# Building rows of `yv` for two more chunks by batch: four column groups in single rounds, and most gather copies on ScalarE

## The chip, the cores and the metric

The kernel runs on one core of a Trainium2 chip. The metric is the device time of one execution in microseconds (us). Two kernels are compared by executions of the same rounds on the same chip. "Span" is the length of one profiled execution, some 2 us shorter than its time.

## The reference, cut to what matters

Causal attention with a decaying bias feeds a spectral mix: 64 Fourier modes of the sequence are multiplied by complex weights of 512 x 512 each, transformed back and added to the input; then comes a product with `w_ch` and a ReLU.

```python
def _moe_ref(x, w_r, w_i, w_ch):               # x is the attention's output, (8, 576, 512)
    X = np.fft.rfft(x, axis=1)
    Xr, Xi = np.real(X[:, :64]), np.imag(X[:, :64])
    Yr = einsum('bmd,mde->bme', Xr, w_r) - einsum('bmd,mde->bme', Xi, w_i)
    Yi = einsum('bmd,mde->bme', Xr, w_i) + einsum('bmd,mde->bme', Xi, w_r)
    y = np.fft.irfft(Y, n=S, axis=1)           # Y holds Yr + 1j*Yi for 64 modes, else 0
    u = x + y
    return u + np.maximum(u @ w_ch, 0.0)
```

(The arrays `w_r` and `w_i`, 64 x 512 x 512 in float32, are most of what is read from memory.)

## The kernel before

The 64 modes go in eight chunks of eight, `c` = 0 to 7. All chunk numbers in this text and in the prediction are these, counted from zero. For the last quarter of the model dimension (`g = NG - 1`) each chunk's modes product gives `y_sb`, 128 rows = 16 real and imaginary modes x 8 batches. The inverse transform needs these rows, and their product with `w_ch`, ordered by mode within a batch: the tile `yv` (128 modes; batch; 0 for y and 1 for y@w_ch; 512). There are two ways to get them there.

By chunk, `y_times_wch`: one product of 128 rows, a copy to `v_sb`, and a transfer of 128 KB that spreads the rows over the batches.

```python
def spread(c, which, rows):
    nc.sync.dma_start(out=yv[16 * c : 16 * c + 16, :, which, :], in_=rows)

def y_times_wch(c, yt):
    vp = auxpool.tile([P, DM], FP32, name="v_ps", tag="aux")     # auxpool: PSUM, 2 buffers
    # ... 4 matmuls of yt (128 x 128) with wch_sb
    vb = spool.tile([P, DM], FP16, name="v_sb", tag="v")
    nc.vector.tensor_copy(out=vb, in_=vp)
    spread(c, 1, vb)
    return vb
```

By batch, `gather`: the transposed rows of several chunks lie in `yt_first`; a matmul takes one batch's columns of them as weights, so its result has the right order already. Several batches stand side by side in column groups of one PSUM tile, and each group is copied into `yv` by itself.

```python
def gather(c0, c1, turns, kinds):
    n = 2 * MC * (c1 - c0)            # 64 rows for chunks 0 to 3, 32 for 4 and 5
    ng = P // n                       # groups side by side: 2 or 4
    for b0 in range(0, B, ng):
        for which in kinds:           # 0: identity, gives y; 1: wch_sb, gives y@w_ch
            ps = auxpool.tile([P, DM], FP32, name="g_ps", tag="aux")
            # ... 4 x ng matmuls with tile_position=(0, n * g)
            for g in range(ng):
                dst, src = yv[rows, b0 + g, which, :], ps[n * g : n * g + n, :]
                if g % 2:
                    nc.vector.tensor_copy(out=dst, in_=src)
                else:
                    nc.scalar.copy(out=dst, in_=src)
        # ... if b0 // ng in turns: work()
```

Before, chunks 0 to 3 go by batch altogether; chunks 4 and 5 go by batch for y alone (identity) and by chunk for y@w_ch; chunks 6 and 7 go by chunk. The order of it (`work()` is an independent product of x with `w_ch`, to fill TensorE):

```python
for c in range(NCK - 2):
    yb = modes(NG - 1, c)
    # ... work(); x_transposed(0) in chunk 5
    yt = y_transposed(yb, c)
    # ... work()
    if c >= NY:                                  # chunks 4 and 5
        y_times_wch(c, yt)
        if c == NCK - 3:
            gather(NY, NCK - 2, (), (0,))
    elif c == NY - 1:
        gather(0, NY, (1, 3), (1, 0))
c = NCK - 2                                      # chunk 6
x_times_wch(0, False)
yb6 = modes(NG - 1, c)
x_transposed(1)
yt = y_transposed(yb6)
x_times_wch(1, False)
vb6 = y_times_wch(c, yt)
# ... chunk 7: modes in four quarters, with first_u and first_z between them
```

The modes product, the transposes, `v_ps` and `g_ps` all use the two buffers of `auxpool`, a pool in PSUM, the memory that the products of TensorE are written to here. Weights stream in all the time through transfers that GpSimd issues; SyncE issues those into `yv` and the results.

The softmax here doesn't subtract the row's maximum and nothing guards it: scores larger than these inputs give would overflow.

## Time and profile before

| what | before |
|---|---|
| time, median of 3 | 456.47 us (455.56 to 456.91) |
| profiled span | 453.8 us (time 455.52) |
| chunk four's modes product starts | 390.79 |
| last quarter of chunk seven's starts | 415.30 |
| from there to the end | 38.50 |

Lines of a time line read: start (us), duration, engine, source line, operation, out<-in, shape in partitions x elements, type, count of instructions in a row; in brackets the idle time ahead of it and who ended it. The prediction below shows TensorE and VectorE of the stretch that is edited. ScalarE's side of the same gather of chunks four and five, which the prediction uses for its spacing:

```profile
402.29 0.57 ACT L664 CAST yv<-g_ps 32x512 f16<-32x512 f32 x1 [0.27 <-PE g_ps L652]
403.61 1.17 ACT L664 CAST yv<-g_ps 32x512 f16<-32x512 f32 x2 [0.75 <-DVE yv L662]
405.66 0.58 ACT L664 CAST yv<-g_ps 32x512 f16<-32x512 f32 x1 [0.88 <-DVE yv L662]
```

Four copies of 32 rows each (one batch's), about 0.58 us apiece; the two in a row took 1.17 together, and between them ScalarE waits for VectorE's copies of the same tile.

### The profile page before, as it was taken

To read this page: it belongs to the slowest core of one execution; us is meant where nothing else is said; L and a number is where in the kernel's file an instruction comes from. 1 tells how busy PE (TensorE), PEld (TensorE's weight loads), DVE (VectorE), ACT (ScalarE), POOL (GpSimd) and SP (SyncE) were. 2 spreads that over 40 slices of the span, in tenths; PEclk is the share of its full clock that TensorE was granted. 3 is DMA by queue.
4 is the path that set the end of the run, shared out by engine and by line. 5 is a ranking of instruction groups with operands and counts; after the bars stand their busy time and mean duration, and the time that the engine had idled before them with its cause. 6 is when DMAs were issued, how large, how long until landed. Compare 5 with 4: busy or idle time off the path is not lost.

```text
span 453.8 us, 10370 instructions
## 1 busy us (share of the span) xinstructions
PE 340.4 (75%) x4233; PEld 218.6 (48%) x4265; DVE 241.0 (53%) x535; ACT 221.9 (49%) x390; POOL 183.0 (40%) x269
## 2 busy tenths in 40 slices
PE   1779887976563979836677857688889678879995
PEld 1456665654342656624445535456554335534332
DVE  7775665753242656723436434446655443562796
ACT  1585877464242656724435444455551323431774
POOL 6655554554344565434364444444433231200000
PEclk9996999998576889968878899889996986999999
DMA  9999999999999999999999999999999999995688
GB/s 176 200 203 203 202 201 204 202 204 204 205 204 202 201 203 202 205 205 204 202 196 203 204 204 203 204 203 202 206 207 208 207 206 206 207 214 109 232 298 317
DMA packets 108511, 93.75 MB, mean 207 GB/s; under 512 B 28384, under 2 KB 103648, under 8 KB 108464
## 3 DMA queue, kind: packets, MB, share of 16 engines
q0 software_dynamic: 98960, 81.81, 113.8%
q1 hardware_dynamic: 9504, 11.29, 7.8%
q8 instruction: 33, 0.54, 0.4%
q14 instruction: 14, 0.11, 0.1%
HBM read 164.56 MB, written 9.44 MB: 383 GB/s over the span
## 4 chain that ended last, share of the span: by engine, by line
DMA 51%; PE 31%; DVE 8%; issue 4%; POOL 2%; ACT 2%; SPq 0%; DVEq 0%; POOLq 0%; ACTq 0%
DMA w_sb<-in_moe_w_i_dram 21%; DMA q<-in_q_dram 15%; DMA w_sb<-in_moe_w_r_dram 11%; PE sc_ps L365 4%; PE av_ps L394 4%; PE z_ps L602 3%; PE yp L441 3%; PE sc_ps L359 3%; PE tr_ps L324 3%; DMA k<-in_k_dram 2%; PE z_ps L693 2%; PE g_ps L652 2%; PE ft_ps L418 2%; PE u_ps L712 2%; PE u_ps L693 1%
## 5 line engine op out<-in xcount | busy, mean ns | idle before, releaser
L373 ACT ACTIVATE p_sb<-sc_ps,cumt_sb 128x576 f16<-128x576 f32 (+1 forms) x256 | 141.7, 635 | 45.6 <-PE sc_ps L365 45.0
L217 POOL DMA_DIRECT2D w_sb<-in_moe_w_i_dram x60 | 45.1, 751 | 85.0 <-PE yp L441 37.6
L217 POOL DMA_DIRECT2D w_sb<-in_moe_w_r_dram x60 | 45.3, 757 | 63.5 <-DMA w_sb<-in_moe_w_r_dram 28.2
L217 POOL DMA_DIRECT2D v<-in_v_dram x72 | 50.8, 708 | 32.0 <-DMA w_sb<-in_moe_w_r_dram 7.4
L324 PE MATMUL tr_ps<-ident,q 64*64 64x64 bf16 x576 | 17.5, 210 | 54.3 <-DMA q<-in_q_dram 54.3
L359 PE MATMUL sc_ps<-negm,ident 128*128 128x256 bf16 x256 | 55.5, 303 | 0.2
L327 DVE COPY qtA<-tr_ps 64x576 bf16<-64x576 bf16 x32 | 23.8, 743 | 49.6 <-PE tr_ps L324 49.5
L441 PE MATMUL yp<-w_sb,xs 128*32 128x512 bf16 x480 | 36.5, 406 | 14.1 <-DMA w_sb<-in_moe_w_i_dram 11.1
L344 ACT ACTIVATE p<-sc_ps,cumt 128x64 f16<-128x64 f32 x32 | 10.0, 313 | 74.3 <-PE sc_ps L340 74.3
L394 PE MATMUL av_ps<-v,p_sb 128*128 128x65 f16 x1024 | 44.5, 198 | 0.0
L394 PEld LDWEIGHTS <-p_sb 128*128 128x128 f16 x1024 | 39.5, 100 | 4.9 <-issue 0.8
L327 DVE COPY ktA<-tr_ps 64x576 bf16<-64x576 bf16 x32 | 24.0, 749 | 33.6 <-PE tr_ps L324 33.6
L324 PEld LDWEIGHTS <-q 64*64 64x64 bf16 x576 | 13.7, 123 | 57.0 <-DMA q<-in_q_dram 56.3
L365 PE MATMUL sc_ps<-qtB,ktB 128*128 128x64 bf16 (+2 forms) x160 | 34.9, 324 | 3.5 <-issue 2.4
L365 PE MATMUL sc_ps<-qtA,ktA 65*128 65x512 bf16 (+2 forms) x192 | 36.5, 299 | 0.7 <-DMA qtA<-ncum_sb 0.7
L399 DVE TENSOR_REDUCE den<-av_ps 128x5 f32<-128x10 f32 x64 | 10.8, 169 | 49.1 <-PE av_ps L394 48.9
L441 PEld LDWEIGHTS <-xs 128*32 128x32 bf16 x512 | 22.6, 170 | 23.8 <-issue 19.8
L404 DVE TENSOR_TENSOR x_all<-av_ps,rcp 128x320 f16<-128x320 f32 x64 | 31.5, 491 | 2.2
L327 ACT COPY ktB<-tr_ps 64x576 bf16<-64x576 bf16 x32 | 20.3, 634 | 20.3 <-DVE ktA L327 19.4
L365 PEld LDWEIGHTS <-ktB 128*128 128x128 bf16 x192 | 22.4, 117 | 14.8 <-issue 6.3
L324 PE MATMUL tr_ps<-ident,k 64*64 64x64 bf16 x576 | 17.3, 209 | 15.3 <-DVE qtB L327 10.7
L602 PE MATMUL z_ps<-wch_sb,xs 128*128 128x512 f16 x96 | 26.1, 421 | 0.2 <-DVE xs L596 0.2
(117 smaller groups left out, 534.8 us busy)
## 6 DMA issues: line engine op xcount, KB each, us to landing
w_sb<-in_moe_w_r_dram POOLq DMA_DIRECT2D x60, 512.0 KB, 11.9
w_sb<-in_moe_w_i_dram POOLq DMA_DIRECT2D x60, 512.0 KB, 11.9
q<-in_q_dram POOLq DMA_DIRECT2D x32, 144.0 KB, 9.9
k<-in_k_dram POOLq DMA_DIRECT2D x32, 144.0 KB, 10.0
v<-in_v_dram POOLq DMA_DIRECT2D x72, 64.0 KB, 9.7
out_dram<-r_sb SPq DMA_DIRECT2D x16, 256.0 KB, 2.2
out_dram<-r_w SPq DMA_DIRECT2D x16, 256.0 KB, 2.6
x_all<-in_moe_w_i_dram POOLq DMA_DIRECT2D x3, 512.0 KB, 9.9
```

The lines of the kernel that those rows point to most:

```text
L217: nc.gpsimd.dma_start(out=dst, in_=src)
L324: nc.tensor.transpose(ps[rows, r, :], src[rows, r, :], ident16[rows, rows])
L327: copy(out=dst[n % NQ][rows, :].rearrange("d (p r) -> d p r", r=R), in_=ps[rows].rearrange("d r p -> d p r"),)
L359: nc.tensor.matmul(ps[:, bass.ds(w * S, W)], ident16, negm[:, bass.ts(r, W)], start=True, stop=False, skip_group_check=True,)
L365: nc.tensor.matmul(ps[:, c0 : c0 + i1 - i0], keys[:, w, r, :], qt[:, i0:i1], start=False, stop=True, skip_group_check=True,)
L373: nc.scalar.activation(out=pt[:, poff[x] : poff[x] + S - w * W], in_=ps[:, w * S : (w + 1) * S - w * W], func=ACTF.Exp, bias=cumt_sb[:, x, ...
L394: nc.tensor.matmul(ps[:, I, r : r + NCH], lhsT, rhs, start=(i == 0), stop=(i == len(todo) - 1), skip_group_check=True,)
L399: nc.vector.tensor_reduce(out=den, in_=ps[:, :, 0 : VW : NCH], axis=mybir.AxisListType.X, op=ALU.add)
L404: nc.vector.tensor_tensor(out=x_all[:, g, b, :, D * h : D * h + D], in0=ps[:, :, 1 : NCH], in1=rcp.unsqueeze(2).to_broadcast([P, NT, D]), ...
L441: nc.tensor.matmul(ps[32 * cg : 32 * cg + 32, :], cols[:, c0 : c0 + 32, c * MC + 2 * cg + par], wt[(g, c, ri, par)][:, cg, :], start=(x == ...
L602: nc.tensor.matmul(z[:, x, :], xts[i][:, x, dt, :], wch_sb[:, dt, :], start=(dt == 0), stop=(last and dt == DT - 1), skip_group_check=True,)
L693: nc.tensor.matmul(dst[x][r, :], G_sb[rows, bass.ds(T * P, r.stop - r.start)], yv[rows, bb, which, :], start=start, stop=True, skip_group_ ...
```

## The change

The intent is to send y@w_ch of chunks four and five the way of the other chunks: by batch, in four column groups, so that two products, two VectorE copies and two transfers of 128 KB go away. The rounds are no longer made in one place but singly, between other products, where TensorE was waiting for `y_sb`. And in every gather only the last copy of a tile is VectorE's, so that VectorE is free for `y_sb`. Cut to its core:

```diff
-    def gather(c0, c1, turns, kinds):
+    def gather(c0, c1, r, which):          # one round r, one kind
...
-                    if g % 2:
+            if g == ng - 1:
                 nc.vector.tensor_copy(out=dst, in_=src)
             else:
                 nc.scalar.copy(out=dst, in_=src)
...
-        if c >= NY:
-            y_times_wch(c, yt)
-            if c == NCK - 3:
-                gather(NY, NCK - 2, (), (0,))
-        elif c == NY - 1:
-            gather(0, NY, (1, 3), (1, 0))
+        if c == NY - 1:
+            for r in range(4):
+                gather(0, NY, r, 1)
+                gather(0, NY, r, 0)
+                if r % 2:
+                    work()
+        elif c == NCK - 3:
+            gather(NY, NCK - 2, 0, 1)
+            gather(NY, NCK - 2, 0, 0)
     c = NCK - 2
     x_times_wch(0, False)
+    gather(NY, NCK - 2, 1, 1)
     yb6 = modes(NG - 1, c)
     x_transposed(1)
+    gather(NY, NCK - 2, 1, 0)
     yt = y_transposed(yb6)
```

More of the change, by code (lines that the diff above doesn't have):

```diff
@@ L645, in gather @@
         ng = P // n
-        for b0 in range(0, B, ng):
-            for which in kinds:
-                ps = auxpool.tile([P, DM], FP32, name="g_ps", tag="aux")
-                for dt in range(DT):
-                    for g in range(ng):
-                        op = yt_first[:, dt, : c1 - c0].rearrange("p c (x b) -> p (c x) b", b=B)
-                        nc.tensor.matmul(
-                            ps[n * g : n * g + n, :] if which else ps[n * g : n * g + n, bass.ts(dt, P)],
-                            op[:, :, b0 + g],
-                            wch_sb[:, dt, :] if which else ident16h,
-                            start=(dt == 0 or not which), stop=(dt == DT - 1 or not which),
-                            tile_position=(0, n * g), skip_group_check=True,
-                        )
-                for g in range(ng):
-                    dst, src = yv[rows, b0 + g, which, :], ps[n * g : n * g + n, :]
-                    if g % 2:
-                        nc.vector.tensor_copy(out=dst, in_=src)
-                    else:
-                        nc.scalar.copy(out=dst, in_=src)
-            if b0 // ng in turns:
-                work()
+        ps = auxpool.tile([P, DM], FP32, name="g_ps", tag="aux")
+        op = yt_first[:, :, : c1 - c0].rearrange("p d c (x b) -> p d (c x) b", b=B)
+        for dt in range(DT):
+            for g in range(ng):
+                nc.tensor.matmul(
+                    ps[n * g : n * g + n, :] if which else ps[n * g : n * g + n, bass.ts(dt, P)],
+                    op[:, dt, :, r * ng + g],
+                    wch_sb[:, dt, :] if which else ident16h,
+                    start=(dt == 0 or not which), stop=(dt == DT - 1 or not which),
+                    tile_position=(0, n * g), skip_group_check=True,
+                )
+        for g in range(ng):
+            dst, src = yv[rows, r * ng + g, which, :], ps[n * g : n * g + n, :]
+            if g == ng - 1:
+                nc.vector.tensor_copy(out=dst, in_=src)
+            else:
+                nc.scalar.copy(out=dst, in_=src)
     ahead = []
```

## The prediction

> **What bounds the kernel now.** I read the page's slices first, then the chain of waits, then the last 80 us engine by engine, then the landing times of the last weight loads.
>
> The page: the DMA engines stand at nine tenths or more from the first slice to slice 36 of 40, and the chain of waits gives 51% of the span to DMA, nearly all of it weight and query loads.
>
> ```profile
> DMA  9999999999999999999999999999999999995688
> DMA 51%; PE 31%; DVE 8%; issue 4%; POOL 2%; ACT 2%; SPq 0%; DVEq 0%; POOLq 0%; ACTq 0%
> ```
>
> So the kernel streams weights until about 415 us, and a tail of some 38 us after that needs no loads. The change touches neither: it sits between chunk four (its modes product starts at 390.79) and the last quarter of chunk seven (415.30). The windows of that stretch (us; PE, PEld, DVE, ACT, POOL busy; clock; DMA share, GB/s):
>
> ```profile
> 390.80:396.10 5.30, 4.49 (x45) 2.39 (x44) 2.62 (x5) 2.38 (x3) 2.97 (x4) 1.00 1.24 207
> 396.10:405.00 8.90, 7.39 (x85) 3.82 (x84) 5.74 (x9) 3.56 (x6) 0.74 (x1) 1.00 1.23 211
> 405.00:411.00 6.00, 4.70 (x40) 2.35 (x40) 3.21 (x5) 1.16 (x2) 0.00 (x0) 1.00 1.23 214
> 411.00:415.80 4.80, 4.78 (x31) 1.83 (x30) 0.69 (x1) 0.00 (x0) 0.00 (x0) 1.00 0.56 116
> ```
>
> TensorE is busy 78 to 85% up to 411 and all of the time from 411 to 415.8, at full clock; that is its in-order stream with a few gaps. TensorE in order of time, cut to what the change touches:
>
> ```profile
> 395.13 1.03 PE L633 MATMUL v_ps<-wch_sb,yt_first 128*128 128x512 f16 x4
> 396.08 1.12 PE L441 MATMUL yp<-w_sb,xs 128*32 128x512 bf16 x16
> ...
> 398.85 0.40 PE L625 MATMUL yt_ps<-ident16h,y_sb 128*128 128x128 f16 x4 [1.09 <-DVE y_sb L455]
> ...
> 402.61 0.47 PE L652 MATMUL g_ps<-ident16h,yt_first 128*32 128x128 f16 x16 [0.38 <-DVE v_sb L637]
> ...
> 407.75 0.40 PE L625 MATMUL yt_ps<-ident16h,y_sb 128*128 128x128 f16 x4 [1.10 <-DVE y_sb L455]
> 408.34 1.90 PE L602 MATMUL z_ps<-wch_sb,xs 128*128 128x512 f16 x8 [0.20 <-DVE xs L596]
> ...
> 415.30 0.47 PE L441 MATMUL yp<-w_sb,xs 128*32 128x512 bf16 x4
> ```
>
> The gaps of 1.1 us are waits for `y_sb`, the modes result copied out by VectorE. Why it is late for chunk six is in VectorE's stream: it is queued behind the gather's copies, which alternate with ScalarE's.
>
> ```profile
> 402.89 0.69 DVE L662 CAST yv<-g_ps 32x512 f16<-32x512 f32 x1 [0.33 <-ACT yv L664]
> 404.22 1.41 DVE L662 CAST yv<-g_ps 32x512 f16<-32x512 f32 x2 [0.64 <-ACT yv L664]
> 406.27 0.69 DVE L662 CAST yv<-g_ps 32x512 f16<-32x512 f32 x1 [0.64 <-ACT yv L664]
> 407.00 0.69 DVE L455 TENSOR_TENSOR y_sb<-yp,y_acc 128x512 f16<-128x512 f32 x1
> ```
>
> Last, the load that the 415.30 product needs. It is issued at 396.87 and lands 18.3 us later, at 415.17, so it is 0.13 us early; the product starts right behind its predecessor. TensorE's order and the DMA stream meet within 0.2 us there. This is the fact the prediction turns on.
>
> ```profile
> 396.87 0.74 POOL L217 DMA_DIRECT2D w_sb<-in_moe_w_i_dram  x1 [2.15 <-PE yp L441]
> w_sb<-in_moe_w_i_dram POOLq DMA_DIRECT2D x1, 512.0 KB, 18.3
> ```
>
> **What the skill says.** The Trainium skill, "TensorEngine Tiling (Array Packing)", Performance Considerations, says that tiling speeds TensorE but not the emptying of PSUM, which may become the bottleneck. The trace agrees: two rounds of 16 identity products took 0.41 us each, their eight copies 402.29 to 406.96. "PSUM — Partial Sum Buffer", PSUM bank collisions, says that two engines on one bank must be kept apart, reads against reads included, though quadrants differ freely. Here the schedule separates them by the whole tile: each VectorE copy above starts after the ScalarE copy of the same tile, although they read different quadrants. "DMA: Bandwidth & Descriptors", Issuing engines are not separate DMA queues, says that transfers from all queues share the same 16 engines; the landings of the weights below agree.
>
> **The change part by part.** Everything up to chunk four keeps its order: the first gather has two groups per round, so its copies are one on ScalarE and one on VectorE as before.
>
> Removed: for chunks four and five, two products of 4 matmuls (next start 0.95 us after the first's start, 0.80 to 0.95 of the path each, say 1.8 us of TensorE), two VectorE copies `v_sb` of 0.69 us, and two SyncE transfers of 128 KB into `yv`.
>
> Added: two rounds of 16 matmuls with 32 weight columns and 512 columns out. The modes product has the same form, x16 in 1.12 us, its successor 1.05 after its start; so 2 x 1.05 = 2.1 us. So TensorE gets 0.3 us more work, not less. Each new round is also emptied by four copies of 32x512: eight more copies. All 16 copies now stand as 12 on ScalarE and 4 on VectorE, that is +8 and 0; with the two `v_sb` gone VectorE saves 1.4 us, ScalarE gains 8 x 0.58 = 4.6 us. ScalarE has 1.16 to 3.56 us of work in windows of 6 to 9 us, so it has room; a tile of four takes 3 ScalarE copies and one VectorE copy behind them. Two ScalarE copies in a row took 1.06 (64x512) and 1.17 us (32x512) together, one alone 0.58, thus they start 0.48 (overlapping) to 0.59 apart; with 0.48 a tile is freed 2 x 0.48 + 0.58 + 0.69, about 2.3 us, after its product is readable.
>
> Moved: rounds one (product, identity) stand before the first late `z_ps` product, round two's product behind it, round two's identity behind chunk six's modes product. All use the same two auxiliary PSUM buffers as the modes product and the transposes, so each waits for the copies of the tile two back.
>
> I put this on one time line, keeping the distances that the trace shows (modes product start to `y_sb` 1.18, `y_sb` to transposes 0.74, `z_ps` product 1.73, its `ScalarE` copy 1.93 after its start):
> - Modes of five start at 395.13, not 396.08 (no `v_ps` before). But VectorE is in the 1.22 us subtraction begun at 396.37, so `y_sb` starts at 397.51, not 398.11, and the transposes at 398.25: 0.6 gained.
> - `z_ps` 398.48 to 400.21; round one's product to 401.26, its identity to 401.67, the next `z_ps` to 403.40. Copies of tile one: ScalarE 401.39 to 402.93, VectorE to 403.66; of tile two: to 405.1.
> - Round two's product waits 0.33 for tile one: 403.73 to 404.78. Chunk six's modes waits 0.39 for tile two: 405.17, against 404.97 before. The gain is used up.
> - Round two's VectorE copy (406.49 to 407.18) is ahead of `y_sb` of six, which starts at 407.09, against 407.00. The identity round hides in that gap (407.25 to 407.66). Transposes 407.83, `z_ps` 408.43, `v_ps` 410.17 (its buffer free 410.02), chunk seven's modes 411.13, against 411.04.
> - From there 4.26 us of solid TensorE work as before: 415.39 against 415.30.
>
> With ScalarE copies 0.59 apart, and thus later releases, the same line gives about 415.8. So TensorE's path: +0.1 to +0.5 us.
>
> The DMA side gains: landings of the last six weight loads are 400.8, 404.28, 406.2, 409.3, 412.0, 415.17, that is 14.37 us for five, where undisturbed ones come each 2.54 us (512 KB at 206 GB/s): 12.7. The 1.67 us extra fit the four 128 KB transfers in that time, about 0.63 us each, the last only partly. Two go away: the last weight lands near 413.9 (estimate), 1.3 us earlier, and nothing is there to use it. It only sets the floor: at best 415.30 - 413.9, thus 1.4 us gained.
>
> After 415.4 nothing differs. Sum: near 0, from -1.4 to +0.5.
>
> **Rivals.** (1) The rounds fill TensorE's waits fully, because copies go faster than I think or the stalls for the buffers vanish: then chunk seven waits for its weights and the gain is capped at 1.3 us: 455.1. For it: all three waits of 1.1 us are there to be filled, and the arrangement looks made for it. Against: two buffers for four more users. (2) ScalarE's serial copies hold the buffers and delay chunk six: +0.5 to +1 us, 457.2. For it: each tile now needs 3 copies of one engine, and they also queue ahead of the copy of chunk six's transposes. Against: ScalarE is only about 40% busy there. (3) Fewer transfers let all weights land earlier and the end moves with them. Against: the product at 415.30 does not wait in the trace.
>
> **Range and chances.** The before runs spread over 455.56 to 456.91, 1.35 us, as much as the whole effect. The middle of my line is +0.1 to +0.5; the first rival pulls the other way by up to 1.3. I take 0.2 us off for the chance of it and set 456.3. The range takes both rivals and half the spread of the runs: 454.8 to 457.4. A change of 2% is 9 us, seven times the cap; faster 0.01, same 0.98, slower 0.01.
>
> **What would show it.** In the changed profile: the start of the last quarter of chunk seven's modes at 415.3 +- 0.6; the last weight landing about 1.3 us before it instead of 0.1; waits of TensorE for `yv` copies in round two and chunk six's modes, 0.3 to 0.4 us each; `y_sb` of five about 0.6 earlier, `y_sb` of six about unchanged; the stretch from there to the end within 0.3 us of 38.5. Wrong would be: that last quarter waiting for its weights (rival 1), a start later than 416 (rival 2), or a difference that arises before 390 us or after 415 us.

## More of the kernel before

Behind the last weight load, the first product that reads all 128 rows of `yv` (`128*128`; earlier ones read 96 rows) follows TensorE's previous work with no wait:

```profile
421.12 1.03 PE L827 MATMUL z_ps<-r_sb,ident16h 128*128 128x512 f16 x4
421.99 0.59 PE L693 MATMUL z_ps<-yv,G_sb 128*128 128x512 f16 x2
```

And two rows of the page's table of DMA queues (packets, MB, share of 16 engines' span), which the prediction passes over and which come back below. The page labels them as instructions, so they are the instructions themselves being fetched: 33 packets of 16 KB on one queue, 14 of 8 KB on another.

```profile
q8 instruction: 33, 0.54, 0.4%
q14 instruction: 14, 0.11, 0.1%
```

## The result, and the profile after

| | before | after |
|---|---|---|
| time, median of 6 of the same rounds | 456.54 us (455.56 to 457.51) | 458.31 us (457.15 to 458.98) |
| ratio, 95% interval | | 1.0037 (1.0018 to 1.0056) |
| profiled span | 453.8 | 454.7 |
| A: chunk four's modes start | 390.79 | 390.02 |
| B: last quarter of chunk seven's starts | 415.30 | 415.15 |
| the stretch, B - A | 24.51 | 25.13 |
| from B to the first product that reads all of `yv` | 6.69 | 7.13 |
| from that product to the end | 31.81 | 32.42 |

A ratio is the mean time of one kernel's runs over that of the other's of the same rounds, so it is not quite the ratio of the medians quoted beside it. The interval excludes 1: the changed kernel is slower by about 1.7 us, above the range of 454.8 to 457.4.

Absolute times mislead here. Up to A the two kernels do the same work in the same order, yet A differs by 0.77 us: it lay between 390.0 and 392.6 over all profiled runs, as the stream of weights comes a little earlier or later. The profiled execution of the changed kernel was also its fastest of six. So everything below is read from A or from B on. The three differences, 0.62 + 0.44 + 0.61, give 1.67 us. (A span is given to 0.1 us, so the times to the end, here and in the table of runs, are good to 0.05.)

**The stretch.** TensorE after:

```profile
397.48 0.40 PE L625 MATMUL yt_ps<-ident16h,y_sb 128*128 128x128 f16 x4 [1.36 <-DVE y_sb L455]
...
400.45 0.42 PE L650 MATMUL g_ps<-ident16h,yt_first 128*32 128x128 f16 x16
400.80 1.90 PE L602 MATMUL z_ps<-wch_sb,xs 128*128 128x512 f16 x8
403.21 1.09 PE L650 MATMUL g_ps<-wch_sb,yt_first 128*32 128x512 f16 x16 [0.50 <-DVE yv L660]
404.98 1.12 PE L441 MATMUL yp<-w_sb,xs 128*32 128x512 bf16 x16 [0.68 <-DVE yv L660]
...
406.87 0.48 PE L650 MATMUL g_ps<-ident16h,yt_first 128*32 128x128 f16 x16 [0.23 <-DVE yv L660]
407.60 0.40 PE L625 MATMUL yt_ps<-ident16h,y_sb 128*128 128x128 f16 x4 [0.25 <-DVE y_sb L455]
```

Chunk five's transposes come 7.46 us after A, before 8.06: the gain of 0.6 is there. Then the bracketed waits for `yv` copies take it back, 0.50 and 0.68 us, and chunk six's transposes come 17.58 after A, before 16.96. ScalarE after, in one line, nine copies back to back:

```profile
400.68 5.41 ACT L662 CAST yv<-g_ps 32x512 f16<-32x512 f32 x9
```

That is 5.41 / 9 = 0.60 us each, with a wait of 0.14 for the third tile's product in it; without one (r8) the nine take 5.29. VectorE after:

```profile
402.46 0.70 DVE L660 CAST yv<-g_ps 32x512 f16<-32x512 f32 x1 [3.84 <-ACT yv L662]
404.23 0.69 DVE L660 CAST yv<-g_ps 32x512 f16<-32x512 f32 x1 [1.07 <-ACT yv L662]
406.12 0.70 DVE L660 CAST yv<-g_ps 32x512 f16<-32x512 f32 x1 [1.20 <-PE yp L441]
406.85 0.69 DVE L455 TENSOR_TENSOR y_sb<-yp,y_acc 128x512 f16<-128x512 f32 x1
```

VectorE is now mostly idle, but its single copy of each tile stands behind three of ScalarE's, and `y_sb` of chunk six stands behind the third of these copies. The row of nine ends at 406.09, VectorE's copy starts at 406.12, `y_sb` at 406.85: 16.83 after A, before 16.21. The difference, 0.62 us, is that of the whole stretch. B hangs on this `y_sb`: it comes 8.3 us after it in the kernel before, after, and in r1, r4, r8 and r10 alike, though `y_sb` itself lies between 15.09 and 18.59 after A.

**Between B and the first product that reads all of `yv`.** TensorE after, against the two lines shown of before:

```profile
420.97 1.03 PE L828 MATMUL z_ps<-r_sb,ident16h 128*128 128x512 f16 x4
422.28 0.60 PE L689 MATMUL z_ps<-yv,G_sb 128*128 128x512 f16 x2 [0.28 <-DMA yv<-v_sb]
```

It comes 1.31 us after its predecessor's start, before 0.87, and waits for the last transfer into `yv`, that of chunk seven's `v_sb`, which neither part of the edit touches. The DMA view from that transfer's issue on, of the kernel after (queue, kind: packets, MB, share; then out<-in, count, KB, us from issue to landing):

```profile
q8 instruction: 1, 0.02, 2.1%
...
yv<-v_sb SPq DMA_DIRECT2D x1, 128.0 KB, 3.7
```

and before, where no instruction packet is in that window:

```profile
yv<-v_sb SPq DMA_DIRECT2D x1, 128.0 KB, 2.9
```

The trace's packets tell more: the fetch started at 419.8 and took one of the 16 DMA engines for 1.2 us; 135 of the transfer's 144 packets had started by 420.47, the last nine only from 421.03 to 421.8. (That these nine are one engine's is inferred: the packed trace doesn't name the engine of a packet.) Before, that fetch came at 423.6.

**The end.** SyncE's waits for DMA in the last microseconds, after and then before (total, times, longest):

```profile
SPq L880 <- DMA out_dram<-r_sb: 2.2, 3, 1.1
```

```profile
SPq L879 <- DMA out_dram<-r_sb: 1.6, 3, 0.6
```

And the DMA view of the last four outputs, after, then before:

```profile
q14 instruction: 1, 0.01, 0.5%
...
out_dram<-r_sb SPq DMA_DIRECT2D x4, 256.0 KB, 2.6
```

```profile
out_dram<-r_sb SPq DMA_DIRECT2D x4, 256.0 KB, 2.1
```

Again a fetch of instructions, this time of the other queue, stands beside the last transfers: at 449.3, after they were issued at 449.01. Before, it came at 446.9, ahead of them (448.70). In the trace after, one engine's share of the last output ends 0.39 us behind the other fifteen (453.01 against 452.62).

The packed trace splits the 0.61 further. The last output took 2.65 us from issue to landing, before 2.16: 0.49. The other 0.12 is no transfer: behind the last landing SyncE went through five more closing waits, 0.06 us apart, where before it had three, so that landing to end took 1.22 us, before 1.10. It was 1.09 or 1.10 in all seven profiles with before's number of transfers issued by SyncE and ScalarE, 1.21 or 1.22 in the seven with two fewer, 0.97 in r13 with two more.

### The profile page after: what moved, and what is told of

It reads as the page before. It is cut to its first block, busy times and chain, and to the rows that moved or that the text cites. A ratio compares the mean times of both kernels' runs of the same rounds, so it can differ in the third digit from the quotient of the medians.

```text
span 454.7 us, 10452 instructions
## 1 busy us (share of the span) xinstructions
PE 344.2 (76%) x4289; PEld 219.2 (48%) x4289; DVE 239.3 (53%) x533; ACT 226.7 (50%) x398; POOL 182.7 (40%) x269
## 4 chain that ended last, share of the span: by engine, by line
DMA 66%; PE 20%; issue 4%; POOL 3%; DVE 3%; ACT 2%; DVEq 0%; POOLq 0%; ACTq 0%
DMA w_sb<-in_moe_w_i_dram 33%; DMA q<-in_q_dram 13%; DMA w_sb<-in_moe_w_r_dram 10%; DMA k<-in_k_dram 4%; DMA v<-in_v_dram 2%; PE yp L441 2%; PE sc_ps L365 2%; PE z_ps L689 2%; PE z_ps L602 2%; DMA y_acc<-in_moe_w_r_dram 2%; DMA y_acc<-in_moe_w_i_dram 2%; PE g_ps L650 2%; PE sc_ps L359 2%; PE tr_ps L324 1%; PE u_ps L708 1%
## 5 line engine op out<-in xcount | busy, mean ns | idle before, releaser
L359 PE MATMUL sc_ps<-negm,ident 128*128 128x256 bf16 x256 | 56.6, 308 | 0.2
L365 PE MATMUL sc_ps<-qtB,ktB 128*128 128x512 bf16 (+2 forms) x192 | 44.4, 349 | 0.0
```

The source lines that it names most:

```text
L359: nc.tensor.matmul(ps[:, bass.ds(w * S, W)], ident16, negm[:, bass.ts(r, W)], start=True, stop=False, skip_group_check=True,)
L365: nc.tensor.matmul(ps[:, c0 : c0 + i1 - i0], keys[:, w, r, :], qt[:, i0:i1], start=False, stop=True, skip_group_check=True,)
```

## The experiments

The theories. For the stretch: (i) the two PSUM buffers of `auxpool`, held by copies, block TensorE; or (ii) the row of copies itself, now two tiles longer, delays `y_sb` of chunk six, whatever buffer it reads; or (iii) the new places of the rounds are bad; or (iv) the new split between ScalarE and VectorE is. For what comes behind B: the fetches of instructions fall on running transfers because the change altered how many instructions each engine's stream holds; the rival is that something of the change itself (later copies, other buffers) delays chunk seven. (The expectations use letters of their own, A to G, and say each time what the letter stands for.) The count is easily told from the diff: TensorE loses 2 x 4 matmuls and gains 2 x 16, each with its weight load, so 2 x (32 - 8) = 48 more; SyncE loses two transfers, VectorE two copies.

All thirteen runs; times are medians, "against" is before in the same rounds. The last three columns are read from the run's profiled execution, as in the table above.

| run | median, against | ratio (95%) | stretch | B to all of `yv` | end |
|---|---|---|---|---|---|
| before (first profile) | | | 24.51 | 6.69 | 31.81 |
| after | 458.31, 456.54 | 1.0037 (1.0018 to 1.0056) | 25.13 | 7.13 | 32.42 |
| r1 after again | 457.94, 455.99 | 1.0038 (1.0026 to 1.0050) | 25.15 | 7.28 | 32.39 |
| r2 copies only | 455.49, 455.99 | 0.9990 (0.9978 to 1.0002) | 24.24 | 6.67 | 31.78 |
| r3 place only | 456.00, 455.99 | 0.9998 (0.9986 to 1.0010) | 25.84 | 6.66 | 31.77 |
| r4 one place | 459.81, 455.99 | 1.0085 (1.0071 to 1.0099) | 26.90 | 7.29 | 32.46 |
| r5 after, 48 more on TensorE | 457.21, 456.01 | 1.0021 (1.0007 to 1.0035) | 25.13 | 6.70 | 32.40 |
| r6 before, 48 more on TensorE | 456.70, 456.01 | 1.0013 (0.9995 to 1.0031) | 24.55 | 6.92 | 32.01 |
| r7 after, 2 more on VectorE | 458.20, 456.01 | 1.0044 (1.0028 to 1.0060) | 25.13 | 6.97 | 32.48 |
| r8 after, other buffers | 458.16, 456.01 | 1.0046 (1.0031 to 1.0062) | 25.01 | 6.77 | 32.41 |
| r9 r5, 2 more on SyncE | 457.57, 456.18 | 1.0016 (0.9997 to 1.0035) | 25.13 | 6.70 | 32.59 |
| r10 after, half the copies | 455.90, 456.18 | 0.9990 (0.9976 to 1.0005) | 23.39 | 7.31 | 32.55 |
| r11 place, transfers deferred | 455.93, 456.18 | 1.0001 (0.9981 to 1.0020) | 24.07 | 7.55 | 31.84 |
| r12 before, 2 fewer on SyncE | 456.58, 456.18 | 0.9998 (0.9977 to 1.0020) | 24.52 | 6.68 | 32.23 |
| r13 r5, 4 more on SyncE | 457.36, 456.18 | 1.0022 (1.0005 to 1.0039) | 25.12 | 6.69 | 31.79 |

One profiled execution isn't the mean of the timed ones, so the three columns do not add up to each ratio. Where A came early and TensorE then waited for weights (r3), the stretch is long without costing time.

### Is it there again? r1

The changed kernel once more, unedited, on another set of rounds.

> The changed kernel once more, to see which differences of the two profiles come back. Theory A (the buffers: TensorE waits for the gather's copies in PSUM): from the start of chunk four's modes product to the last quarter of chunk seven's again about 25.1 us (before: 24.5), with waits of 0.5, 0.7, 0.2 us for yv copies; the ratio to before is 1.002 to 1.005. Theory B (the tail: the last transfer into yv lands later): from that quarter to the end again about 39.5 us (before 38.5), with a wait for that transfer. Theory C (chance of the clock before chunk four): the stretch starts at a place that changes by 1 us between runs of the same kernel, and neither of the two differences comes back.

Ratio 1.0038, and all three differences are back: 25.15, 7.28 (a wait of 0.42), 32.39. They are the kernel's, not the execution's.

### Which part of the change? r2, r3, r4

r2 is the kernel before with the new split of the copies alone:

```diff
-                    if g % 2:
+                    if g == ng - 1:
```

> Only the copies: the kernel before with three of four 32-row copies on ScalarE. Theory A: fewer changes of engine free each buffer about 0.3 us earlier, chunk six's copy out starts up to 0.5 us earlier, ratio 0.998 to 1.000, stretch 24.0 to 24.5 us. Theory B: two transfers are still there, tail as before, 38.5. If the copies on ScalarE are themselves the cost: ratio 1.002 or more.

Ratio 0.9990, its interval just including 1. The split alone does no harm to the eight copies of the kernel before, so (iv) falls for them. How sixteen copies would fare with half of them on each engine was not tested.

r3 has the new split and the new places for the identity rounds, but y@w_ch of chunks four and five by chunk as before, against the changed kernel:

```diff
-        elif c == NCK - 3:
-            gather(NY, NCK - 2, 0, 1)
-            gather(NY, NCK - 2, 0, 0)
+        if c >= NY:
+            y_times_wch(c, yt)
+            if c == NCK - 3:
+                gather(NY, NCK - 2, 0, 0)
...
-    gather(NY, NCK - 2, 1, 1)
     yb6 = modes(NG - 1, c)
```

> Chunks four and five keep their products by chunk (and their transfers), only the identity rounds are placed singly as in the changed kernel, copies mostly on ScalarE. Theory A: two copies' rounds fewer, no wait for a buffer of over 0.2 us, stretch about 24.0 to 24.4 us, ratio 0.997 to 1.000. Theory B: transfers as before, tail 38.5. If the placement of rounds between products is the cost: stretch 25 us.

Ratio 0.9998, so (iii) falls too. TensorE of r3 shows something more: its last quarters now wait for weights.

```profile
413.29 0.45 PE L441 MATMUL yp<-w_sb,xs 128*32 128x512 bf16 x4 [1.11 <-DMA w_sb<-in_moe_w_i_dram]
...
416.17 0.45 PE L441 MATMUL yp<-w_sb,xs 128*32 128x512 bf16 x4 [0.58 <-DMA w_sb<-in_moe_w_i_dram]
```

With two more such waits (0.28 and 0.29) that is 2.3 us in which TensorE has nothing to do: the new places do fill its gaps, and the landing of the last weights (416.1 here, 415.17 before) is what it meets instead. Both parts by themselves cost no time that these runs can tell; what is left is the third, the products by batch.

r4 is the changed kernel with all four rounds made one after another behind chunk five:

```diff
             gather(NY, NCK - 2, 0, 1)
             gather(NY, NCK - 2, 0, 0)
+            gather(NY, NCK - 2, 1, 1)
+            gather(NY, NCK - 2, 1, 0)
...
-    gather(NY, NCK - 2, 1, 1)
     yb6 = modes(NG - 1, c)
     x_transposed(1)
-    gather(NY, NCK - 2, 1, 0)
```

> All four rounds (products in groups and identities) directly after chunk five, none later. Theory A: the rounds wait for each other's copies in a row: two waits of about 1.2 us more than when spread out, stretch 26 to 27 us, ratio 1.004 to 1.008. Theory B: no transfers for chunks four and five, tail as in the changed kernel (39.5). If buffers do not matter: as the changed kernel.

Ratio 1.0085, a stretch of 26.90 and waits of 2.34 and 0.68 us for `yv` copies. Spreading the rounds is what makes the products by batch nearly affordable: it is worth 1.0085 - 1.0037, about 2.2 us of 456.

### Buffers or copies? r8 and r10

r8 takes the first two tiles of the late gather from another PSUM pool:

```diff
-        ps = auxpool.tile([P, DM], FP32, name="g_ps", tag="aux")
+        late_first = c0 == NY and r == 0
+        pool, tag = (upool, "u") if late_first else (auxpool, "aux")
+        ps = pool.tile([P, DM], FP32, name="g_ps", tag=tag)
```

> The changed kernel with the first round's two tiles in the PSUM pool of the transposes, which is idle then; nothing else. Theory A (the buffers held by the serial copies cost the stretch its 0.6 us): the waits of 0.5 and 0.7 us for yv copies go, chunk six's modes product starts 1.0 to 1.2 us earlier, and the stretch falls from 25.1 to 24.0 to 24.3 us or until it waits for the last weights (about 414.5); tail as in the changed kernel (39.5). Ratio 1.001 to 1.003. If the stalls are not what costs: stretch 25.1, ratio 1.0038.

The waits of 0.50 and 0.68 are gone, and chunk six's modes product starts 13.52 us after A instead of 14.96. The stretch is still 25.01 and the ratio 1.0046. TensorE of r8, and then its VectorE:

```profile
408.33 0.48 PE L652 MATMUL g_ps<-ident16h,yt_first 128*32 128x128 f16 x16 [1.39 <-DVE yv L662]
```

```profile
408.31 0.69 DVE L455 TENSOR_TENSOR y_sb<-yp,y_acc 128x512 f16<-128x512 f32 x1
```

One wait of 1.39 stands in place of two, and `y_sb` of chunk six comes 408.31 - 391.61 = 16.70 after A, against 16.83. The modes product that it reads (405.13, 1.04 long) was done two microseconds earlier; it was the copies that it stood behind. Theory (i) falls: the freed buffers bring 0.12 us.

r10 keeps the buffers and leaves two of the three ScalarE copies of each late tile out. The values that they would bring are missing (the rows are zeroed early instead); the comparison with the reference did not notice it, so it says nothing about this kernel.

```diff
         for g in range(ng):
             dst, src = yv[rows, r * ng + g, which, :], ps[n * g : n * g + n, :]
+            if ng == 4 and g in (1, 2):
+                continue
```

> Wrong result on purpose: of the four copies of each late tile only the first (ScalarE) and the last (VectorE) are made, the rest of yv is zeroed early; products and buffers as in the changed kernel. Theory F (the row of nine copies on ScalarE, 0.60 us each, then VectorE's own copy ahead of y_sb of chunk six, sets the stretch): y_sb of six starts 2 us earlier or more, the waits for yv copies go, and the stretch falls from 25.1 to 23.5 or to where it waits for the last weights (landing about 414.5). If the grouped products themselves cost it: stretch 25.

ScalarE's first two copies in r10, TensorE's modes product of chunk six (no wait in brackets ahead of it), and VectorE's `y_sb`:

```profile
401.71 1.05 ACT L668 CAST yv<-g_ps 32x512 f16<-32x512 f32 x2
...
404.58 1.03 PE L441 MATMUL yp<-w_sb,xs 128*32 128x512 bf16 x16
...
406.14 0.69 DVE L455 TENSOR_TENSOR y_sb<-yp,y_acc 128x512 f16<-128x512 f32 x1
```

No wait of TensorE for a copy into `yv` is left in the stretch, `y_sb` of chunk six comes at 406.14, 15.09 after A, and the stretch is 23.39: 1.74 shorter than after and 1.12 shorter than before. With r8, which freed the buffers and kept the copies, this shows the row of copies, theory (ii), as the cause of the 0.62 us; with half of the copies the stretch would have had the gain that the change was after. Whether it is their number or ScalarE's twelve of sixteen was not separated, nor was `y_sb` placed ahead of the copies in VectorE's order. The last weights land at 414.35 and TensorE starts B at 414.44, within 0.1 of them.

### The fetches of instructions: r5, r6, r7

24 tiny matmuls, with their weight loads 48 instructions, far ahead in the program, into a tile that is written again later. r5 is the changed kernel with them, r6 the kernel before:

```diff
         ct_ps = cpsum.tile([P, NK + 1, NPAIR], FP32, name="ct_ps")
+        for _ in range(24):
+            nc.tensor.matmul(ct_ps[:32, 0, :32], p4[1][:, NL : NL + 32], p4[1][:, NL : NL + 32],
+                             start=True, stop=True, skip_group_check=True)
```

> The changed kernel with 24 tiny products (48 TensorE instructions) added in the first 10 us, where TensorE waits. Theory D (the changed kernel's 48 more TensorE instructions move a 16 KB instruction fetch onto the last transfer into yv): the fetch comes about 3.8 us earlier relative to the work, near 416, the last transfer into yv takes 2.9 us again instead of 3.7, no wait for it on TensorE, from chunk seven's last quarter to the end 0.4 us less (39.1). Theory B (fewer transfers themselves make the last one slow): 3.7 us and the wait as before. The stretch stays 25.1 either way.

> The converse: the kernel before with the same 24 tiny products early. Theory D: the fetch that came at 423.6 comes near 420, on the last transfer into yv, which takes about 3.7 us; TensorE waits 0.3 to 0.4 us for it; tail 38.5 -> 38.9, ratio 1.0005 to 1.0015. Theory B: 2.9 us, no wait, tail 38.5, ratio 1.000.

r5, the DMA view from the issue of the last transfer into `yv` on; no instruction packet is in it, the fetch came at 415.6:

```profile
yv<-v_sb SPq DMA_DIRECT2D x1, 128.0 KB, 2.9
```

The same view of r6, whose fetch came at 420.0 instead of 423.6:

```profile
q8 instruction: 1, 0.02, 2.1%
...
yv<-v_sb SPq DMA_DIRECT2D x1, 128.0 KB, 3.5
```

The 48 instructions take the wait away from the changed kernel (6.70, with no wait) and bring it to the kernel before (6.92). This is shown both ways in the traces. Over all profiles it holds too: in the seven with this fetch 1.1 to 1.3 us behind its issue (after, r1, r4, r6, r7, r8, r10) the last transfer into `yv` took 3.3 to 3.9 us, in the seven without it 2.9 to 3.0 (r11, with its other order of transfers, apart). In time r5 fell from about 1.0037 to 1.0021, but the intervals overlap; r6 rose to 1.0013, with an interval that includes 1.

r7 adds two small memsets on VectorE to the changed kernel, as many as the copies that VectorE lost:

```diff
-    nc.vector.memset(zero, 0.0)
+    for _ in range(3):
+        nc.vector.memset(zero, 0.0)
```

> The changed kernel with two more tiny VectorE instructions at the very start (it has two fewer than before). Theory E (VectorE's 8 KB instruction fetch lands on the last output transfers in the changed kernel): that fetch comes some 2 us earlier relative to the work, near 447, the last outputs land 0.4 to 0.6 us earlier, the end's wait for them falls from 2.2 to 1.6 us; the ratio to before falls by 0.001 from 1.0038. If the fetch is another engine's (SyncE's, which has two transfers fewer): fetch stays at 449 and the wait at 2.2.

The end stays at 32.48 with a longest wait of 1.1: the fetch beside the last outputs is not VectorE's.

### The end: r9, r12, r13

SyncE is the other engine that lost two instructions of its own. r9 is r5 with two tiny transfers on SyncE at the start, r13 the same with four:

```diff
     nc.sync.dma_start(out=G_sb, in_=d_G)
+    spare = gp.tile([P, 2, 16], FP32, name="spare")        # r13: 4 in place of 2
+    for i in range(2):
+        nc.sync.dma_start(out=spare[:, i, :], in_=d_ident32[:, :16])
```

> The changed kernel with both instruction streams set back: 48 early TensorE instructions, and two tiny SyncE transfers (128 rows of 64 bytes) in the first microseconds, for the two that the change removed. Theory D with SyncE as the owner of the 8 KB fetch at 449 us: that fetch comes about 2 us earlier relative to the work, the end's wait for the last outputs falls from 2.2 to 1.6 us, the last transfer into yv takes 2.9 us, the tail is 38.5 us as before; the stretch stays 25.1, so the ratio is that of the stretch alone, about 1.0015. If the fetch is not SyncE's: tail 39.1, ratio 1.002.

r9 was a miss: two transfers moved the fetch, but only to 449.2, still less than a microsecond ahead of the outputs issued at 449.93, and the end took 32.59. So the count of transfers put back is not by itself what restores it. By the trace the fetch now met earlier outputs, and the delay carried on: the one issued at 447.94 took 2.86 us (2.26 in r5, 2.25 in r13 below), the last one 2.95. Why that is more than after's 2.65 stays open.

> The changed kernel with the 48 early TensorE instructions and four tiny early SyncE transfers; two of them moved the 8 KB fetch by 1.0 us only, and it still fell beside the last outputs. Theory D for the end: the fetch comes 2 us or more before the last four outputs are issued, the last piece falls from 32.4 to 31.8 us, tail 38.5, ratio 1.0015 or below. If the fetch has nothing to do with it: 32.4 us, tail 39.1.

With four, the fetch came at 447.9 and the outputs were issued at 450.12. SyncE's waits at r13's end:

```profile
SPq L886 <- DMA out_dram<-r_sb: 1.6, 3, 0.6
```

These are the kernel before's numbers, to the digit. The end is 31.79 and the whole tail 38.48, before 38.50. That it is so exact is in part luck: the last output took 2.30 us, against 2.66 in r5 and 2.16 before, and the 0.14 that is missing is made good by the closing waits (0.97 from landing to end, before 1.10). The ratio, 1.0022, does not show the gain over r5's 1.0021: the intervals, some 0.3% wide, are wider than the 0.13% that 0.6 us make, and the four transfers are extra work of their own. So the gain is shown in the trace, not in the times.

r12 is the converse, the kernel before with two of SyncE's early loads issued by ScalarE:

```diff
-    nc.sync.dma_start(out=ident16h, in_=d_ident16h)
-    nc.sync.dma_start(out=G_sb, in_=d_G)
+    nc.scalar.dma_start(out=ident16h, in_=d_ident16h)
+    nc.scalar.dma_start(out=G_sb, in_=d_G)
```

> The converse for the end: the kernel before with two of its early constant loads issued by ScalarE, so that SyncE has two transfers fewer, as in the changed kernel; no work is changed. Theory D for the end: SyncE's 8 KB fetch comes near 449 instead of 447, beside the last outputs, and the piece from the first full product of the second stage (the one that reads all of yv) to the end is 32.4 us as in the changed kernel, not 31.8; the longest wait of the end for outputs is 1.1, not 0.6 us; ratio 1.001. If the number of SyncE's transfers is not the cause: 31.8 and 0.6, ratio 1.000.

The fetch came at 450.1, 0.39 us behind the issue of the fifth output from the end (449.71) and ahead of the last four (issued from 450.49); before, it was 0.98 us ahead of that fifth output. r12's last output took 2.65 us, as in the changed kernel, where before's took 2.16; its closing waits are before's (1.10 from landing to end), as is the number of transfers that SyncE and ScalarE issue together. The end took 32.23, where 32.4 was expected. The longest single wait for an output stayed 0.6 (four waits, 2.1 in all), where 1.1 was expected: that sign was missed. The time, 0.9998, does not tell. The converse is shown in the trace, for the whole of the transfer's 0.49 us.

Over all fifteen profiles the last output took 2.16 to 2.35 us in the six in which this fetch started 0.6 us or more ahead of the issue of the fifth output from the end (before, r2, r3, r6, r11, r13), and 2.65 to 2.95 in the nine in which it started after it.

### A version that is faster? r11

r3 left TensorE waiting for weights, so r11 takes traffic out of the way of them: chunk six's two transfers into `yv` are issued behind chunk seven's first.

```diff
     yb = modes(NG - 1, NCK - 1, {2: first_u, 3: first_z})
+    spread(NCK - 2, 0, yb6)
+    spread(NCK - 2, 1, vb6)
```

> A version that may beat both: products of chunks four and five by chunk, identity rounds placed singly (that kernel waited for weights: last landing 416.1), and the two transfers of chunk six issued only behind chunk seven's first, when the weights are through. Theory G (the stretch's floor is the landing of the last weights, and each 128 KB transfer in that time moves it by 0.5 us or more): last weights land 0.7 to 1.3 us earlier, near 415, the stretch ends there, tail 38.5; ratio 0.997 to 0.999. If the deferred transfers then delay the last one into yv: a wait for it of 0.3 us or more in the tail.

B came 24.07 after A with two waits for weights left (0.67 and 0.30), but the deferred transfers then stood in the way of chunk seven's last: it took 4.1 us (the deferred one ahead of it 4.2), and the first product of all of `yv` waited 0.72 for it (7.55). Ratio 1.0001. What was saved ahead of B was paid behind it.

No version that I ran is clearly faster than the kernel before: r2 and r10 are at 0.9990, both intervals include 1, and r10 computes a wrong result.

## Why the prediction was wrong

Predicted 456.3 us, with 454.8 to 457.4; measured 458.31. "Same" at 2% held; the range did not.

- **The step that failed: "After 415.4 nothing differs."** The tail was to be within 0.3 us of 38.5 and took 39.55 (39.67 in r1), 1.05 more: 0.44 in front of the first product of all of `yv` and 0.61 at the end. Without that the time would have been 457.26, within the range given. The prediction named "a difference that arises before 390 us or after 415 us" as what would make it wrong. It looked for effects through data and buffers, and there are none behind B. It did not count instructions: 48 more for TensorE and two transfers fewer for SyncE move the fetches of their streams onto transfers that the end waits for (0.44 and 0.49), and two transfers fewer leave two more closing waits behind the last landing (0.12). In other words, 1.05 of the 1.67 us stood in no term of the sum. That the fetches are those of TensorE (16 KB) and SyncE (8 KB) is inferred from which edits moved them (r5, r6; r13, r12; not r7).
- **The stretch: right mechanism, a term too small.** +0.1 to +0.5 were predicted, +0.62 came. The term is the spacing of ScalarE's copies: 0.48 or 0.59 were offered, and the row of nine had 0.60. The line with 0.59 gave about 415.8, thus +0.5, close to what came; the middle of the range lay on the other. The 0.48 was taken from two 64x512 copies, which read the same rows of two successive tiles. It isn't the shape: two 32x512 copies placed so in r10 took 1.05, also 0.48 apart, while those of one tile, which read different rows, start 0.585 apart in every run. The predicted waits of 0.33 and 0.39 were 0.50 and 0.68. TensorE's own work was put 0.1 us too high for each product round (1.05; the next instruction starts 0.92 after it), so it gets no more work than before; that helped and was not enough.
- **Where it comes from was half right.** The prediction's line had the gain used up by tiles whose buffers are late. Both waits are such, but r8 takes them away and nothing is gained: `y_sb` of chunk six is behind the copies themselves. That step was in the line too, as 407.09 against 407.00, where 0.62 later was measured.
- **Chunk five's `y_sb` 0.6 earlier: right** (6.72 after A, before 7.32). B at 415.3 +- 0.6 was met too (415.15), though partly because A came 0.77 early.
- **The last weight load 1.3 us earlier: about two thirds.** In nine profiles with two transfers fewer (after, and all its variants but r3 and r11) the last weight landed between 413.56 and 414.74, middle 414.5; in five with all four transfers (before, r2, r3, r6, r12) between 415.01 and 416.14, middle 415.4. That is 0.9 us (in the pair profiled first, B came 0.4 us behind the last landing, in r1 1.8, where 1.3 was to show it), and it stays unused, as predicted, because TensorE came later.
- **The rivals.** Rival 2, ScalarE's row of copies with "+0.5 to +1 us, 457.2", is what happened in the stretch, at its lower edge, though not by the buffers that it put first (r8) but by what stands in the queue. Rival 1 did not come: the gaps were there to be filled (r3 filled them, r10 went below before's stretch), but not with eight more copies. Rival 3 was rightly dismissed.

What stays open: why some of the runs' times differ from the sum of their three columns by more than half a microsecond (r3, r8, r10). One profile per kernel can't settle that.

## What to carry to other kernels

Making a product in the layout in which it is needed saves its transfer, but if it is then emptied in four pieces, count the pieces: eight more copies of 0.60 us on one engine cost more in the stretch here than two products, two copies and two transfers had cost. When an engine is put ahead of another's urgent instruction, ask what stands in that engine's queue in order, not how busy it is: VectorE was nearly idle and still late, because each of its copies followed three of ScalarE's. And where an edit adds or removes instructions, a few tenths of a microsecond can arise far from it, where a fetch of instructions now meets a transfer that something waits for; add harmless instructions far ahead before blaming the edit's own logic.

## What the Trainium skill lacked or had wrong

- "Runtime: NRT & Kernel Launch", Instruction fetch mechanics, says that instructions come in blocks of 16 KiB (256 instructions) over a DMA queue of the sequencer's own and that the cost of crossing a block is "mostly hidden". The trace has packets of that size on one queue (33 packets, 0.54 MB); those of the other are half as large (14 packets, 0.11 MB, so 8 KB each). What the page lacks is another cost: where the last transfer into `yv` was fetched over, TensorE shows no wait for instructions, but 128 KB took 3.7 us instead of 2.9, 0.44 us on the path, and at the end the last output 2.65 instead of 2.16. No page that I read says that a fetch can delay a data transfer in this way, or that 48 instructions more or less can decide which.
- "PSUM — Partial Sum Buffer", PSUM bank collisions, lets two engines read different quadrants of a bank at the same time. This kernel's schedule did not use that: VectorE's copy of a quadrant started only behind ScalarE's of the same tile (402.46, 404.23, 406.12, each with ScalarE's copies as what it waited for or stood behind). The section has no word on what ordering by whole tiles costs; here it puts three copies of 0.60 us in front of VectorE's one.
- No page that I read says that the spacing of ScalarE's copies from PSUM depends on what follows what: 0.48 us where both read the same rows of successive tiles (64x512 in every gather of chunks 0 to 3, 32x512 once, in r10), 0.585 to 0.60 where the next one reads other rows (32x512). What sets it was not tested.
